# A block product scheme for one projection, weight sums on another engine, and an order between two engines' sums

## Chip, core and metric

The kernel runs on one core of a Trainium2 chip. The metric is device microseconds of one execution of the program. Three runs of the kernel before gave 254.39, 254.42 and 254.69 us, median 254.42.

## What is computed

```python
B, T, D, K, U = 2, 4000, 512, 5, 8
h = sum of K shifted einsums of x with w1;  h = gelu(h)[:, ::2, :]
f = sum of K shifted einsums of h with w2;  f = gelu(f)[:, ::2, :]
fe = jnp.einsum("btd,de->bte", f, w_f)
ge = jnp.einsum("bud,de->bue", g, w_g)
j = jnp.tanh(fe[:, :, None, :] + ge[:, None, :, :])
return jnp.einsum("btud,dv->btuv", j, w_o)
```

Two convolutions of five taps with stride 2 turn 4000 steps into 1000 per batch. The projected f (512 columns, "fe") is added to each of 8 projected rows of g, tanh is taken, and the product with w_o gives the output of 2 × 1000 × 8 × 512 values, the joint. Inputs and output are bf16.

## The kernel before

Channels lie on the 128 partitions in NK = 4 slices, time along the columns. Batch 0 is convolved first, then batch 1; the convolutions use sums of inputs and weights, so that fewer products are wanted, and each unit (one slice of 128 output channels of one stretch of time) runs through five steps s1 to s5 of one or two products. f of batch b is `fT[b]`, in three planes of NT3 = 334 columns (time modulo 3).

**The projection.** `fe(b, half, m)` takes 501 columns of f and one slice of 128 output channels: four matmuls into one PSUM bank, then one copy to `feT[b]` in float32, by VectorE (L810) for even m and by ScalarE (L480) for odd m. Batch 0 has eight such groups, which run one after another, with a tanh put behind each pair. `tanh` (ScalarE) reads all 1000 columns of one slice of `feT` and adds a column of `geT` as bias; it writes `jT` or, later, `jX`.

**The joint.** The output is made in 28 blocks of class `Seven` (four tiles of 128 rows each) and 13 single tiles of class `Plain`. `Seven` treats a block as a 2 × 2 product of halves and makes it from seven block products for eight: four sums of tanh blocks (`sums`, L980, tile `ss`), four sums of blocks of w_o (`wosums`, tile `tw`), seven products of four matmuls, three of whose accumulated states are kept in float32 (`sn`, L917 and L918) and added again on VectorE at the end (`og`, L475). The sums of w_o are made on GpSimd. Each sum in `sums` may go to VectorE or GpSimd, and evictions written with `evict(None, ...)` may go to ScalarE or VectorE.

**The order.** Instructions are noted as operations with reads, writes and a cost. `Plan.schedule` then lists them per engine: each engine takes an operation that is ready, TensorE and GpSimd the one noted first, VectorE and ScalarE the one with the earliest due time, and up to 150 changed due times are tried against the planner's own end. The order of the text is thus a priority, not an order of execution. `port` marks sums for which VectorE and GpSimd are taken to lock each other out: `lock` is the time at which the last one ends. Waits are put between engines as semaphores in `emit`, from the reads and writes, and from a list `after` of further operations.

**Pieces.** When the first projection is due, steps of batch 1's convolution are left: `conv` holds 26 of them (three of the unit at hand, fifteen of three more units, and the eight groups `fe(1, ...)`). `piece(n)` notes the next n. Before, one piece stands ahead of the first projection and three behind it; then the blocks of the joint take them by `fill`: two each in blocks 0 to 8, one each in 9 to 14, where there are any left.

**The start.** `turn` transposes a first part of x on TensorE; each call's two halves of the result are copied out to `eo`, the first by VectorE (L592), the second by ScalarE. `w1part` makes sums of the first convolution's weights on VectorE (`wu`, `ws`, `ssum`).

Of the kernel before, what the change touches and what calls it, by code (L numbers as in the profile page):

```python
# [10 lines left out]
FP16 = mybir.dt.float16  # L11
# [57 lines left out]
class Plan:  # L69
# [158 lines left out]
    def once(self, pred, succ, late, hold):  # L228


        ops, HOP, n = self.ops, self.HOP, len(self.ops)
        left = [len(p) for p in pred]
        ready = list(hold)
        free = {e: 0.0 for e in ("pe", "act", "dve", "pool", "sp")}
        cand = {e: [] for e in free}
        engines = [o.alt or (o.eng,) for o in ops]
        for i in range(n):
            if not left[i]:
                for e in engines[i]:
                    cand[e].append(i)  # L240
        order, where = {e: [] for e in free}, {}
        wire, lock, start, done = 0.0, 0.0, [0.0] * n, [0.0] * n
        for _ in range(n):
            best = None
            for e, c in cand.items():
                if c:
                    t = max(free[e], min(ready[i] for i in c))
                    if best is None or t < best[0]:
                        best = (t, e)
            t, e = best  # L250
            now = [i for i in cand[e] if ready[i] <= t + 0.02]
            i = min(now) if e in ("pe", "sp", "pool") else min(now, key=lambda i: (late[i], i))
            for f in engines[i]:
                cand[f].remove(i)
            order[e].append(i)
            o = ops[i]
            cost = o.cost
            if o.alt:
                where[i], cost = e, o.alt[e][1]
            start[i] = t  # L260
            free[e] = t + cost
            if o.port:
                if lock > t - 0.2 and e == "dve":
                    free[e] = max(t, lock) + cost + 0.2
                elif lock > t:
                    free[e] = lock + cost
                lock = free[e]
            done[i] = end = free[e]
            if o.dma:
                wire = max(wire, t + 1.8) + o.wire  # L270
                end = max(wire, t + 2.0) + o.slack
            for s in succ[i]:
                ready[s] = max(ready[s], end + HOP if pred[s][i] else free[e])
                left[s] -= 1
                if not left[s]:
                    for f in engines[s]:
                        cand[f].append(s)
        return max(free.values()), order, start, done, ready, where

    def emit(self, block, tail):  # L280
        nc, ops = self.nc, self.ops
        pred = self.edges()
        order = self.schedule(pred)
        pred = self.edges()
        pos = {i: p for e in order for p, i in enumerate(order[e])}
        deps = []
        for o in ops:
            need = {}
            for j, w in pred[o.idx].items():
                q = ops[j]  # L290
                if not w:
                    continue
                if q.dma:
                    need[("dma", j)] = j
                elif q.eng not in need or pos[need[q.eng]] < pos[j]:
                    need[q.eng] = j
            deps.append(need)
            for k, j in need.items():
                if not isinstance(k, tuple):
                    ops[j].signal = True  # L300
        cnt = {e: 0 for e in self.COMPUTE}
        sem = {e: nc.alloc_semaphore(f"s_{e}") for e in self.COMPUTE}
        for e in self.COMPUTE:
            for i in order[e]:
                if not ops[i].dma:
                    if ops[i].signal:
                        cnt[e] += 1
                    ops[i].count = cnt[e]

        def run(name, e):  # L310
            seen = {}

            def wait(s, v):
                if seen.get(id(s), 0) < v:
                    seen[id(s)] = v
                    e.wait_ge(s, v)

            for i in order[name]:
                o = ops[i]
                for k, j in sorted(deps[i].items(), key=lambda kj: -kj[1]):  # L320
                    if isinstance(k, tuple):
                        wait(ops[j].sem, ops[j].val)
                    else:
                        wait(sem[k], ops[j].count)
                ins = o.fn(e)
                if o.dma:
                    ins.then_inc(o.sem, 16)
                elif o.signal:
                    ins.then_inc(sem[name], 1)
            if name == "sp":  # L330
                for s, v in tail:
                    wait(s, v)

        @block.sync
        def _(e):
            run("sp", e)

        @block.gpsimd
        def _(e):
            run("pool", e)  # L340

        @block.tensor
        def _(e):
            run("pe", e)

        @block.scalar
        def _(e):
            run("act", e)

        @block.vector  # L350
        def _(e):
            run("dve", e)


def bass_standalone__seq2seq_rnn_t_joint__speech_kernel(
# [40 lines left out]
    with ExitStack() as es:  # L396
# [62 lines left out]
        assert ss[3].end <= xs[2].end and ss[7].end <= xs[1].end  # L459
        tw = at("tw", [4, 2, NT // 2], FP16, wg_sb.end - wg_sb.bytes)  # L460
        assert tw.end <= wg_sb.end
        ps = Psum(es.enter_context(nc.psum_tensor("acc", [P, 8 * NT], FP32)))
        block = es.enter_context(nc.Block(no_gpsimd_drain=True))
        pl = Plan(nc)
        sub, add = ALU.subtract, ALU.add

        def vec_cost(o, ins, fast=True):
            bf = fast and all(not v.psum and v.ap.dtype == BF16 for v in (o,) + tuple(ins))
            return o.ap.free_size() * (0.52e-3 if bf else 1.04e-3) + 0.065

        def memset(v):
# [2 lines left out]
        def tt(eng, o, a, b, op):  # L474
            pl.op(eng, lambda e: e.tensor_tensor(out=o.ap, in0=a.ap, in1=b.ap, op=op), (a, b), (o,),  # L475
                  0.02 + 2.14e-3 * o.ap.free_size() if eng == "pool" else vec_cost(o, (a, b)))
# [98 lines left out]
        def turn(rt, pp, cost):  # L575
            for h in range(2):
                bk = 4 * (rt ^ pp) + 2 * h + 1
                pv = View(psb[:, bk * 1024:bk * 1024 + 512].rearrange("p (r k c) -> p r k c", r=2, k=2), np.array([bk]), True)

                def fn(e, pv=pv, h=h):  # L580
                    for k in range(2):
                        for r in range(2):
                            ins = e.transpose(pv.ap[:, r, k, :], xr[rt].h[:, 2 * r + pp, 2 * h + k, :], ident.h[:, :])
                    return ins
                pl.op("pe", fn, (xr[rt][:], ident[:]), (pv,), cost)
                lo = 16 + 2 * P * rt
                o = eo[pp, 2 * h:2 * h + 2, lo:lo + 2 * P].map(lambda a: a.rearrange("p k (c r) -> p k c r", r=2))
                v = pv.map(lambda a: a.rearrange("p r k c -> p k c r"))
                if h:
                    act(o, v, ACT.Copy)  # L590
                else:
                    pl.op("dve", lambda e, o=o, v=v: e.tensor_copy(out=o.ap, in_=v.ap), (v,), (o,), vec_cost(o, (v,)))  # L592
# [208 lines left out]
        def fe(b, half, m):  # L801
# [7 lines left out]
            else:  # L809
                pl.op("dve", lambda e, o=o, v=v: e.tensor_copy(out=o.ap, in_=v.ap), (v,), (o,), vec_cost(o, (v,)))  # L810

        def slot(j):
            if j < XB:
                return jT, j % RING
            j = (j - XB) % (WIDE + RING)
            return (jX, j) if j < WIDE else (jT, j - WIDE)
# [23 lines left out]
                act(jcols(k, lo, n), feT[b][k, t:t + n], ACT.Tanh, bias=geT[k * BU + v:k * BU + v + 1])  # L840
                lo += n

        def wosums():
            h = NT // 2
            b11, b12, b21, b22 = (wo_sb[2 * k:2 * k + 2, c * h:(c + 1) * h] for k in range(2) for c in range(2))
            tt("pool", tw[0], b12, b11, sub)
            tt("pool", tw[1], b22, tw[0], sub)
            tt("pool", tw[2], b22, b12, sub)
            tt("pool", tw[3], b21, tw[1], sub)

        def tail_zero(b):
            v = hT[b][2:6, :, HOFF + NT3 - 1:HOFF + NT3]
# [9 lines left out]
        def steps(slot, i, lo, hi):  # L862
            when(slot, *[lambda w=w: trip[i].step(w) for w in STEPS[lo:hi]])
# [18 lines left out]
        when(17, load_late, lambda: tail_zero(1))  # L882
        steps(18, 5, 0, 4)
        steps(19, 5, 4, 13)
        when(20, ge)
        nu = 21
        for t in range(nu):
# [195 lines left out]
                    conv.pop(0)()  # L1083
                    far[0] = not conv

        wosums()
        first = [lambda h=h, m=m: fe(0, h, m) for m in range(NK) for h in range(2)]
        piece()
        for i, f in enumerate(first):
            f()  # L1090
            if i % 2:
                tanhs(0, 0, 1)
        piece(3)

        S1 = 15
        gaps = (1, 3, 5, 7)
# [78 lines left out]
```

## Time and profile before

| what | value |
|---|---|
| median of three runs | 254.42 us |
| profiled execution, its own time | 253.94 us |
| its span, first to last instruction | 252.2 us |
| granted TensorE clock | 1.00 |
| TensorE busy | 246.4 us |
| VectorE busy | 209.9 us |
| ScalarE busy | 210.0 us |
| GpSimd busy | 103.2 us |

PE is TensorE's matmuls, PEld its weight loads, DVE VectorE, ACT ScalarE, POOL GpSimd. Rows of a timeline give start, duration, engine, line, operation, out<-in, shapes and count; a bracket holds the idle time of the engine before it and what ended that. Since matmuls are pipelined, the spacing of their starts, not their duration, is what one of them takes of TensorE.

### The profile page before, as it was taken

The page shows a single profiled execution, that of the slowest core. Times are in us where ns is not written, and L with a number is a line of the kernel's source. Part 1 is how long each engine was busy: PE and PEld are TensorE (multiplying, and loading weights), DVE is VectorE, ACT ScalarE, POOL GpSimd, SP SyncE. Part 2 cuts the span into 40 slices and gives each one's busy share as a digit, 9 for nine tenths or more (in the row PEclk, how much of TensorE's full clock was granted, in tenths as well). Part 3 has the DMA queues.
Part 4 walks back from the last instruction along what each step waited for, and adds up shares of the span by engine and source line. Part 5 has one row for each costly group of instructions (what it writes and reads, how often), then busy time and mean ns, then how long its engine had stood idle before and what let it go on. Part 6 is the DMA issues. An engine that isn't in the chain of part 4 may idle for free.

```text
span 252.2 us, 5270 instructions
## 1 busy us (share of the span) xinstructions
PE 246.4 (98%) x1913; PEld 180.9 (72%) x1919; DVE 209.9 (83%) x342; ACT 210.0 (83%) x352; POOL 103.2 (41%) x107
## 2 busy tenths in 40 slices
PE   7999999999999999999999999999999999999994
PEld 3745977666666666667467878877778878787882
DVE  2699999956999998295546799799899999999783
ACT  4396998859869767884699999999999999998762
POOL 1000000000000000002418889698998999998500
PEclk9999999999999999999999999999999999999999
DMA  6999999989100043000002223332344446555646
GB/s 233 306 229 188 172 142 179 187 148 358 45 0 3 0 143 110 0 1 3 0 0 86 83 87 99 130 108 83 118 137 149 145 135 205 165 167 170 205 149 209
DMA packets 55159, 31.99 MB, mean 127 GB/s; under 512 B 32062, under 2 KB 54878, under 8 KB 55134
## 3 DMA queue, kind: packets, MB, share of 16 engines
q1 hardware_dynamic: 54846, 31.47, 47.6%
q8 instruction: 15, 0.25, 0.4%
q10 hardware_dynamic: 288, 0.20, 0.3%
q14 instruction: 10, 0.08, 0.1%
HBM read 7.86 MB, written 16.38 MB: 96 GB/s over the span
## 4 chain that ended last, share of the span: by engine, by line
PE 87%; DVE 5%; DMA 4%; ACT 1%; issue 1%; SPq 0%; DVEq 0%
PE acc L488 87%; DMA w_sb<-in_w_dram 4%; DVE wu L595 1%; DVE row L475 1%; DVE xa L475 1%; DVE ssum L475 1%; DVE w_t L475 1%; DVE og L475 1%; ACT row L480 0%; DVE w_x L475 0%; ACT w_x L480 0%; ACT sd L480 0%; ACT hT L480 0%; SPq L511 0%; ACT ost L480 0%
## 5 line engine op out<-in xcount | busy, mean ns | idle before, releaser
L475 DVE TENSOR_TENSOR og<-acc,sn 128x512 bf16<-128x512 f32 x84 | 55.6, 683 | 6.4 <-PE acc L488 4.4
L480 ACT ACTIVATE jT<-feT,geT 128x1000 bf16<-128x1000 f32 (+6 forms) x56 | 52.7, 1016 | 0.5 <-DVE feT L810 0.4
L488 PE MATMUL acc<-tw,ss 128*128 128x256 f16 x336 | 46.0, 273 | 0.0
L488 PE MATMUL acc<-row,w_sb 128*128 128x334 bf16 (+2 forms) x224 | 38.8, 296 | 0.0
L488 PEld LDWEIGHTS acc<-tw,ss 128*128 128x128 f16 x336 | 32.6, 98 | 7.8 <-ACT sn L917 0.4
L917 ACT ACTIVATE sn<-acc 128x512 f32<-128x512 f32 x54 | 34.8, 657 | 3.8 <-PE acc L488 3.5
L980 POOL TENSOR_TENSOR ss<-jT 128x512 f16<-128x512 bf16 x23 | 28.8, 1263 | 13.4 <-ACT jT L480 10.8
L488 PE MATMUL acc<-wo_sb,jT 128*128 128x256 bf16 (+1 forms) x187 | 31.5, 292 | 0.3
L488 PEld LDWEIGHTS acc<-row,w_sb 128*128 128x128 bf16 x224 | 21.0, 97 | 8.9 <-DVE acc L595 0.4
L480 ACT ACTIVATE jX<-feT,geT 128x1000 bf16<-128x1000 f32 (+4 forms) x28 | 26.2, 986 | 0.0
L472 POOL MEMSET hT<- 128x8 bf16 (+2 forms) x6 | 0.8, 148 | 61.6 <-ACT hT L480 44.1
L480 ACT ACTIVATE hT<-acc 128x334 bf16<-128x334 f32 (+3 forms) x36 | 15.5, 441 | 9.7 <-PE acc L488 9.7
L488 PEld LDWEIGHTS acc<-wo_sb,jT 128*128 128x128 bf16 x192 | 18.7, 98 | 6.2
L595 DVE SCALAR_TENSOR_TENSOR acc<-acc,sd 128x334 f32<-128x334 f32 (+2 forms) x24 | 11.6, 483 | 13.8 <-PE acc L488 13.7
L480 ACT ACTIVATE sd<-acc 128x334 f32<-128x334 f32 (+2 forms) x48 | 20.4, 433 | 3.2 <-PE acc L488 2.4
L918 DVE COPY sn<-acc 128x512 f32<-128x512 f32 x30 | 20.5, 685 | 2.4 <-PE acc L488 2.4
L475 DVE TENSOR_TENSOR row<-row 128x1336 bf16<-128x1336 bf16 (+2 forms) x24 | 19.0, 795 | 0.0
L980 POOL TENSOR_TENSOR ss<-jX 128x512 f16<-128x512 bf16 x15 | 17.4, 1171 | 1.2 <-ACT jX L480 0.6
L488 PE MATMUL acc<-hT,w_t 128*128 128x334 bf16 x96 | 17.6, 304 | 0.0
L488 PE MATMUL acc<-xp,w_t 128*128 128x334 bf16 (+1 forms) x96 | 17.4, 305 | 0.0
L488 PE MATMUL acc<-xp,w_x 128*128 128x334 bf16 (+1 forms) x96 | 16.9, 305 | 0.0
L488 PE MATMUL acc<-eo,w_sb 128*128 128x468 bf16 (+2 forms) x96 | 16.2, 328 | 0.6 <-ACT eo L480 0.6
(111 smaller groups left out, 511.2 us busy)
## 6 DMA issues: line engine op xcount, KB each, us to landing
out_dram<-og SPq DMA_DIRECT2D x98, 128.0 KB, 2.0
w_sb<-in_w_dram SPq DMA_DIRECT2D x10, 512.0 KB, 5.5
out_dram<-ost SPq DMA_DIRECT2D x10, 128.0 KB, 2.2
xr<-in_x_dram SPq DMA_DIRECT2D x2, 512.0 KB, 4.6
wf_sb<-in_w_f_dram SPq DMA_DIRECT2D x1, 512.0 KB, 3.6
wg_sb<-in_w_g_dram SPq DMA_DIRECT2D x1, 512.0 KB, 4.6
wo_sb<-in_w_o_dram SPq DMA_DIRECT2D x1, 512.0 KB, 5.7
xp<-in_x_dram SPq DMA_TRANSPOSE x18, 4.9
```

What stands on the lines that cost most here:

```text
L472: pl.op("pool", lambda e: e.memset(v.ap, 0.0), (), (v,))
L475: pl.op(eng, lambda e: e.tensor_tensor(out=o.ap, in0=a.ap, in1=b.ap, op=op), (a, b), (o,), 0.02 + 2.14e-3 * o.ap.free_size() if eng == "po ...
L480: pl.op("act", lambda e: e.activation(o.ap, i.ap, func, scale=scale, bias=0.0 if bias is None else bias.ap), rd, (o,), o.ap.free_size() * ...
L488: ins = e.matmul(o.ap, lhsT=l.ap, rhs=r.ap, start=start and n == 0, stop=stop and n == len(pairs) - 1, skip_group_check=not check)
L595: pl.op(eng, lambda e: e.scalar_tensor_tensor(out=o.ap, in0=a.ap, scalar=f, in1=b.ap, op0=ALU.mult, op1=add), (a, b), (o,), vec_cost(o, (a ...
L917: pl.flex({"act": (lambda e: e.activation(o.ap, v.ap, ACT.Copy), 0.05 + n * 0.833e-3), "dve": (lambda e: e.tensor_copy(out=o.ap, in_=v.ap) ...
L918: "dve": (lambda e: e.tensor_copy(out=o.ap, in_=v.ap), 0.065 + n * 1.04e-3)}, (v,), (o,))
L980: fn = lambda e, o=S[i], x=x, y=y, op=op: e.tensor_tensor(out=o.ap, in0=x.ap, in1=y.ap, op=op)
```

## The change

Batch 0's projection becomes two objects of class `FeSeven`, t = 0 and 1, each for two slices of the output (t and t + 2) and all 1002 columns in two overlapping halves of 504: seven products of two matmuls. It needs four sums of f (`fsums`, tile `sf`) and four of w_f (`wsums(twf, wf_sb)`), all on VectorE; three accumulated states per object are kept in float32 (`kf`) by `evict(None, ...)`, and three of four blocks are finished by an addition on VectorE. The sums of w_o move from GpSimd to VectorE by the same function. Nine pieces stand around the first projection: two ahead, three between the objects' products, four behind. In the planner, an engine's own sums no longer lock that engine, and sums of 16-bit floats cost VectorE less. Each port operation of GpSimd also waits for the latest port operation of VectorE that the plan starts up to 1.5 us before it. One of the copies to `eo` goes from VectorE to ScalarE.

```diff
-                if lock > t - 0.2 and e == "dve":
+                if owner != e and lock > t - 0.2 and e == "dve":
                     free[e] = max(t, lock) + cost + 0.2
-                elif lock > t:
+                elif owner != e and lock > t:
                     free[e] = lock + cost
-                lock = free[e]
+                lock, owner = free[e], e
...
+        near = None
+        for o in sorted((o for o in ops if o.port), key=lambda o: (self.start[o.idx], o.eng == "pool")):
+            if o.eng == "dve":
+                near = o.idx
+            elif near is not None and self.start[near] > self.start[o.idx] - 1.5:
+                o.after.append(near)
...
+        QH = NT3 // 2 + 1
+        twf = at("twf", [4, 2, NT // 2], FP16, wv[2].end - wv[2].bytes)
+        sf = at("sf", [4, 2, 3, QH], BF16, xt_off + 8192)
+        kf = [at(f"kf{i}", [3, QH], FP32, v.end - v.bytes) for i, v in enumerate(ssum + ws[:2])]
...
-            bf = fast and all(not v.psum and v.ap.dtype == BF16 for v in (o,) + tuple(ins))
+            bf = fast and all(not v.psum and v.ap.dtype in (BF16, FP16) for v in (o,) + tuple(ins))
...
-                if h:
+                if h or rt and pp:
                     act(o, v, ACT.Copy)
...
+        def fsums(b):
+            a = lambda r, k: fhalf(b, r, slice(2 * k, 2 * k + 2))
+            pl.port = True
+            tt("dve", sf[0], a(1, 0), a(1, 1), add)
+            tt("dve", sf[1], sf[0], a(0, 0), sub)
+            tt("dve", sf[2], a(0, 0), a(1, 0), sub)
+            tt("dve", sf[3], a(0, 1), sf[1], sub)
+            pl.port = False
...
+            def product(self, i, bk, start):
...
+                mm(ps.cols(bk * NT, 3 * QH), [(lhs(k), rhs(k)) for k in range(2)], start, True, False)
...
+            def p1(self):
+                self.A = take()
+                self.product(1, self.A, True)
+                self.s1 = self.keep(self.A)
...
+            def p6(self):
+                self.product(6, self.A, False)
+                self.u2 = self.keep(self.A)
+            def p7(self):
+                self.product(7, self.A, False)
+                self.out(1, 1, self.A, self.d5)
...
+            def p4(self):
+                self.product(4, self.A, False)
+                self.out(1, 0, self.A)
+                free.append(self.A)
...
-        def wosums():
+        def wsums(tw, w):
...
-            tt("pool", tw[0], b12, b11, sub)
...
+            tt("dve", tw[0], b12, b11, sub)
...
+        when(18, lambda: wsums(twf, wf_sb))
...
-        wosums()
-        first = [lambda h=h, m=m: fe(0, h, m) for m in range(NK) for h in range(2)]
-        piece()
-        for i, f in enumerate(first):
-            f()
-            if i % 2:
-                tanhs(0, 0, 1)
+        piece(2)
+        f0, f1 = FeSeven(0, 0), FeSeven(0, 1)
+        f0.p1()
+        f0.p2()
+        fsums(0)
+        wsums(tw, wo_sb)
+        f1.p1()
+        f0.p5()
+        f1.p2()
+        f0.p6()
+        f1.p5()
+        f0.p7()
+        f0.p3()
+        f0.p4()
+        tanhs(0, 0, 1)
         piece(3)
+        f1.p6()
+        f1.p7()
+        f1.p3()
+        f1.p4()
+        tanhs(0, 0, 3)
+        piece(4)
```

More of the change, by code (lines that the diff above doesn't have):

```diff
@@ L241, in once @@
         order, where = {e: [] for e in free}, {}
-        wire, lock, start, done = 0.0, 0.0, [0.0] * n, [0.0] * n
+        wire, lock, owner, start, done = 0.0, 0.0, None, [0.0] * n, [0.0] * n
         for _ in range(n):
@@ L461, in bass_standalone__seq2seq_rnn_t_joint__speech_kernel @@
         assert tw.end <= wg_sb.end
+        QH = NT3 // 2 + 1
+        twf = at("twf", [4, 2, NT // 2], FP16, wv[2].end - wv[2].bytes)
+        sf = at("sf", [4, 2, 3, QH], BF16, xt_off + 8192)
+        kf = [at(f"kf{i}", [3, QH], FP32, v.end - v.bytes) for i, v in enumerate(ssum + ws[:2])]
+        assert twf.end <= wv[3].end and sf.end <= xt[0].end and 3 * QH <= NT
         ps = Psum(es.enter_context(nc.psum_tensor("acc", [P, 8 * NT], FP32)))
@@ L810, in fe, with fhalf @@
                 pl.op("dve", lambda e, o=o, v=v: e.tensor_copy(out=o.ap, in_=v.ap), (v,), (o,), vec_cost(o, (v,)))
+        def fhalf(b, r, k):
+            q0 = r * (NT3 - QH)
+            return fT[b][k, :, q0:q0 + QH]
+        def fsums(b):
[6 more added lines that the diff above has]
+            pl.port = False
@@ new lines, in bass_standalone__seq2seq_rnn_t_joint__speech_kernel, with __init__, keep, out @@
+        class FeSeven:
+            def __init__(self, b, t):
+                self.b, self.t = b, t
+            def product(self, i, bk, start):
+                h, lo = NT // 2, self.t * P
+                rhs = {1: lambda k: fhalf(self.b, 0, k), 2: lambda k: fhalf(self.b, 0, 2 + k),
+                       4: lambda k: fhalf(self.b, 1, 2 + k)}.get(i)
+                if rhs is None:
+                    si = {5: 0, 6: 1, 7: 2, 3: 3}[i]
+                    rhs = lambda k: sf[si, k]
+                lhs = {1: lambda k: wf_sb[k, lo:lo + P], 2: lambda k: wf_sb[2 + k, lo:lo + P],
+                       3: lambda k: wf_sb[2 + k, h + lo:h + lo + P]}.get(i)
+                if lhs is None:
+                    ti = {5: 0, 6: 1, 7: 2, 4: 3}[i]
+                    lhs = lambda k: twf[ti, k, lo:lo + P]
+                mm(ps.cols(bk * NT, 3 * QH), [(lhs(k), rhs(k)) for k in range(2)], start, True, False)
+            kept = 0
+            def keep(self, bk):
+                v = kf[FeSeven.kept % len(kf)]
+                FeSeven.kept += 1
+                evict(None, v[:].map(lambda a: a.rearrange("p r q -> p (r q)")), ps.cols(bk * NT, 3 * QH))
+                return v
+            def out(self, r, c, bk, v=None):
+                q = NT3 // 2
+                cut = lambda a: a[:, :, r:r + q].rearrange("p r q -> p q r")
+                p = ps.cols(bk * NT, 3 * QH).map(lambda a: cut(a.rearrange("p (r q) -> p r q", r=3)))
+                o = feT[self.b][2 * c + self.t, 3 * r * q:3 * (r + 1) * q].map(lambda a: a.rearrange("p (q r) -> p q r", r=3))
+                if v is None:
+                    evict(None, o, p)
+                else:
+                    tt("dve", o, p, v[:].map(cut), add)
+            def p1(self):
+                self.A = take()
+                self.product(1, self.A, True)
+                self.s1 = self.keep(self.A)
+            def p2(self):
+                bk = take()
+                self.product(2, bk, True)
+                self.out(0, 0, bk, self.s1)
+                free.append(bk)
+            def p5(self):
+                self.D = take()
+                self.product(5, self.D, True)
+                self.d5 = self.keep(self.D)
+            def p6(self):
[4 more added lines that the diff above has]
+                self.out(1, 1, self.A, self.d5)
+            def p3(self):
+                self.product(3, self.D, False)
+                self.out(0, 1, self.D, self.u2)
+                free.append(self.D)
+            def p4(self):
+                self.product(4, self.A, False)
+                self.out(1, 0, self.A)
+                free.append(self.A)
@@ L841, in tanh @@
                 lo += n
-        def wosums():
+        def wsums(tw, w):
             h = NT // 2
-            b11, b12, b21, b22 = (wo_sb[2 * k:2 * k + 2, c * h:(c + 1) * h] for k in range(2) for c in range(2))
-            tt("pool", tw[0], b12, b11, sub)
-            tt("pool", tw[1], b22, tw[0], sub)
-            tt("pool", tw[2], b22, b12, sub)
-            tt("pool", tw[3], b21, tw[1], sub)
+            b11, b12, b21, b22 = (w[2 * k:2 * k + 2, c * h:(c + 1) * h] for k in range(2) for c in range(2))
+            pl.port = True
+            tt("dve", tw[0], b12, b11, sub)
+            tt("dve", tw[1], b22, tw[0], sub)
+            tt("dve", tw[2], b22, b12, sub)
+            tt("dve", tw[3], b21, tw[1], sub)
+            pl.port = False
         def tail_zero(b):
```

## The prediction

> **What bounds the kernel now.** I read the page's busy times first, then TensorE's waits, then busy time by stretch, and last the timeline around the projection, at the start, and at the sums.
>
> ```profile
> PE 246.4 (98%) x1913; PEld 180.9 (72%) x1919; DVE 209.9 (83%) x342; ACT 210.0 (83%) x352; POOL 103.2 (41%) x107
> PEclk9999999999999999999999999999999999999999
> PE acc L488 <- DVE zero L495: 1.2, 1, 1.2
> PE acc L488 <- ACT eo L480: 0.6, 2, 0.4
> PE acc L488 <- ACT sd L480: 0.3, 1, 0.3
> ```
>
> TensorE is busy for 246.4 of 252.2 us at full clock, and only 2.1 us of its waiting has a name, all before 28 us. By stretch (duration, then busy time and count of PE, PEld, DVE, ACT, POOL, then clock, DMA share, GB/s):
>
> ```profile
> 117.00:120.50 3.50, 3.50 (x39) 2.50 (x38) 0.01 (x1) 1.25 (x4) 2.19 (x2) 1.00 0.00 0
> 120.50:130.00 9.50, 9.50 (x53) 4.94 (x51) 4.08 (x7) 7.87 (x12) 2.35 (x3) 1.00 0.00 0
> 130.00:140.00 10.00, 9.95 (x78) 7.45 (x77) 7.64 (x14) 10.00 (x17) 7.80 (x7) 1.00 0.16 54
> 140.00:160.00 20.00, 20.00 (x168) 15.90 (x166) 18.13 (x28) 19.64 (x35) 17.82 (x16) 1.00 0.29 93
> 160.00:180.00 20.00, 20.00 (x160) 15.30 (x158) 17.64 (x29) 20.00 (x33) 16.74 (x15) 1.00 0.37 119
> 180.00:200.00 20.00, 20.00 (x172) 16.42 (x170) 19.21 (x32) 20.00 (x32) 18.59 (x17) 1.00 0.39 125
> 200.00:220.00 20.00, 19.84 (x163) 16.04 (x165) 18.74 (x31) 20.00 (x34) 19.94 (x18) 1.00 0.53 172
> 220.00:240.00 20.00, 19.95 (x172) 16.67 (x171) 17.91 (x29) 16.98 (x28) 15.35 (x14) 1.00 0.55 179
> ```
>
> From 117 to 240 us TensorE idles for 0.26 us (0.05, 0.16 and 0.05). So every matmul less is worth its own spacing, and there is nothing else to win there. But ScalarE is full from 130 to 220 us (0.36 us idle of 90), VectorE idles 8.6 us there, and GpSimd is full from 200 to 220. All four engines run abreast: TensorE has the end, with a small margin to the others. Work added to ScalarE and VectorE must therefore go where they have room, which is 117 to 130 us: VectorE idles 3.49 + 5.42 = 8.9 us there and ScalarE 2.25 + 1.63 = 3.9.
>
> **The projection.** These are its rows, with what stands before and behind it (start, duration):
>
> ```profile
> 119.41 0.45 ACT L480 ACTIVATE fT<-acc 128x334 bf16<-128x334 f32 x1 [0.93 <-PE acc L488]
> 120.35 6.99 PE L488 MATMUL acc<-fT,wf_sb 128*128 128x501 bf16 x32
> 121.52 1.42 DVE L810 COPY feT<-acc 128x501 f32<-128x501 f32 x2
> 122.97 1.13 ACT L480 ACTIVATE jT<-feT,geT 128x1000 bf16<-128x1000 f32 x1 [0.39 <-DVE feT L810]
> 127.17 0.73 PE L488 MATMUL acc<-row,w_sb 128*128 128x334 bf16 x4
> 127.74 0.73 PE L488 MATMUL acc<-hT,w_sb 128*128 128x334 bf16 x4
> 130.01 0.38 PE L488 MATMUL acc<-wo_sb,jT 128*128 128x256 bf16 x2
> ```
>
> The 32 matmuls begin at 120.35 and the next work at 127.17: 6.82 us, 213 ns each. The change has 2 × 7 × 2 = 28, of 504 columns: 213 × 504 / 501 = 214.4 ns, together 6.00 us. That is 0.82 us less on the path that sets the end. The Trainium skill, TensorE: Matmul & The Clock Gate, Back-to-back issue gap, gives a sustained spacing of about 131 ns for 512 columns; four fewer would then bring an estimated 0.52 us. The 213 ns here disagree, and I keep 0.82.
>
> **What VectorE and ScalarE get.** Costs come from these groups (last but one: busy us, mean ns):
>
> ```profile
> L475 DVE TENSOR_TENSOR og<-acc,sn 128x512 bf16<-128x512 f32 x84 | 55.6, 683 | 6.4 <-PE acc L488 4.4 <-ACT sn L917 1.7
> L480 ACT ACTIVATE jT<-feT,geT 128x1000 bf16<-128x1000 f32 x32 | 36.3, 1191 | 0.4 <-DVE feT L810 0.4
> L917 ACT ACTIVATE sn<-acc 128x512 f32<-128x512 f32 x54 | 34.8, 657 | 3.8 <-PE acc L488 3.5 <-DVE og L475 0.3
> L475 DVE TENSOR_TENSOR row<-row 128x1336 bf16<-128x1336 bf16 x16 | 13.5, 850 | 0.0
> L475 DVE TENSOR_TENSOR w_t<-w_sb 128x512 bf16<-128x512 bf16 x12 | 5.0, 419 | 0.0
> ```
>
> Each row block reads PSUM seven times, 14 in all against 8: six more VectorE additions of 504 columns at 683 × 504 / 512 = 672 ns, 4.0 us; the other eight cost what the eight copies cost. The four sums of f have 1008 elements; between 419 ns (512) and 850 ns (1336) that is 0.68 us each, 2.7 us. The eight sums of w_f and w_o are 512 long: 8 × 0.42 = 3.4 us. Together 10.1 us, in 12.8 us of room. The sums of w_o leave GpSimd:
>
> ```profile
> 118.31 2.27 POOL L475 TENSOR_TENSOR tw<-wo_sb 128x512 f16<-128x512 bf16 x2 [17.37 <-PE acc L488]
> 120.54 2.39 POOL L475 TENSOR_TENSOR tw<-wo_sb,tw 128x512 f16<-128x512 bf16 x2
> ```
>
> That was idle time of GpSimd: its 2.35 us between 120.5 and 130 are these sums and nothing else, so nothing is won. They cannot start before the g projection has let go of the buffer, which is when GpSimd began, 118.3; VectorE idles from 117 to 120.5, so they and those of w_f fit there. Cost: nothing; without that cover they would stand 3.4 us ahead of the sums of f.
>
> The sums of f wait for the last block of f, out at 119.41 + 0.45 = 119.86 (their buffer lies on planes that the convolution's last products read, which are done by then), and end near 119.9 + 2.7 = 122.6. TensorE arrives at the first of them (product 5) later than now by one more convolution piece: two groups of four, 0.57 us apart as 127.17 and 127.74 show, 1.13 us. So it starts the projection at 121.5, and product 5 after three products of 0.43, at 122.8. The first sum is ready at 120.6. No stall.
>
> **The joint's start.** Nine convolution pieces stand in and around the projection for four. The five more are four pieces of two groups and one of one, 4 × 1.13 + 0.57 = 5.1 us that TensorE does earlier. Now the first full tanh runs at 122.97, because copies of blocks come out one after another. In the new order a block is complete only after product 4, behind the chain product 6, eviction, product 7, addition, product 4, eviction: 3 × (0.43 + 0.17 to the result + 0.67 + 0.1) = 4.1 us from 123.6, so 127.7 us. It begins 4.7 us later, while the first joint product moves from 130.01 by 5.1 − 0.8 to 134.3. The lead shrinks only by about 0.4 us, plus what pieces and evictions take from ScalarE between; I take one tanh of 1.1 us. The second row block starts three pieces (2.8 us) behind the first, is complete near 132.4, and two tanhs are wanted from it: 134.7 against 134.3. TensorE takes the lowest ready number, so other pieces can fill this. Bounds: 0 to 1.1 us; I take 0.3, as the 0.26 us idle of now is the nearest row.
>
> **The start of the kernel.** One copy of turned x goes from VectorE to ScalarE.
>
> ```profile
> 14.00:28.00 14.00, 13.57 (x101) 8.50 (x100) 14.00 (x30) 11.67 (x25) 0.35 (x3) 1.00 0.99 201
> 8.07 1.29 DVE L592 COPY eo<-acc 128x512 bf16<-128x512 bf16 x2 [1.93 <-PE acc L583]
> 10.70 0.69 DVE L595 SCALAR_TENSOR_TENSOR wu<-w_sb,wu 128x512 f32<-128x512 bf16 x1
> 11.43 0.63 ACT L480 ACTIVATE w_x<-wu 128x512 bf16<-128x512 f32 x1 [2.06 <-DVE wu L595]
> 24.95 0.27 PEld L488 LDWEIGHTS acc<-row,w_x 128*128 128x128 bf16 x4 [0.36 <-ACT sd L480]
> 27.24 0.27 PEld L488 LDWEIGHTS acc<-row,w_t 128*128 128x128 bf16 x4 [0.50 <-ACT sd L480]
> ```
>
> VectorE gets half of 1.29, 0.65 us, back; ScalarE has 2.06 us idle before 11.43. From 14 to 28 us VectorE has no pause at all (14.00 of 14), and TensorE, idle for 0.43 us of it, waits at 24.95 and 27.24 for sums that ScalarE copies from that work. Bounds 0 and 0.6 us (VectorE moves by 0.65 at most); I take 0.3, between the two, and no loss, because ScalarE idles where the copy goes.
>
> **GpSimd behind VectorE.** All joint sums by engine, and three meetings:
>
> ```profile
> 126.00:240.00 114.00, 21.31 (x30) 96.24 (x82) 1.00 0.39 126
> 134.51 0.43 DVE L980 TENSOR_TENSOR ss<-jT 128x512 f16<-128x512 bf16 x1 [0.57 <-ACT jT L480]
> 134.55 1.39 POOL L980 TENSOR_TENSOR ss<-jT 128x512 f16<-128x512 bf16 x1 [0.89 <-ACT jT L480]
> 152.17 1.16 POOL L980 TENSOR_TENSOR ss<-ss,jT 128x512 f16<-128x512 f16 x1
> 152.21 1.40 DVE L980 TENSOR_TENSOR ss<-jT,ss 128x512 f16<-128x512 bf16 x1
> ```
>
> The 30 sums on VectorE took 21.31 us; at the 0.43 of the undisturbed one they would take 12.9, so 8.4 us are waiting. At 152.17 GpSimd was 40 ns ahead and VectorE's sum took 1.40, 0.97 too long. The new wait turns such a meeting round: VectorE regains up to 0.97, GpSimd and the sums queued behind it (and the products 5, 6, 7 and 3 that read them) come about 0.5 later. Where VectorE is first anyway, as at 134.51, GpSimd was already held (1.39 for 1.16), and the semaphore's way is added, 0 to 0.2 us. The Trainium skill, SBUF — State Buffer, SBUF: two separate sides, says that the one that starts first keeps the shared ports for its whole instruction; by that rule the wait can pay only in such races, not in every meeting, and both pairs agree with it. On the path I put this at zero: bounds −0.5 (VectorE's regained time removes the small gaps) and +0.5 (GpSimd has 0.06 us spare from 200 to 220).
>
> **Sum.** 253.94 − 0.82 − 0.30 + 0.30 = 253.1 us for the profiled execution. It lies 0.48 us under the median of 254.42, so the median becomes 253.6, 0.32% less. The measurement tells about 0.2%, 0.5 us.
>
> **Rivals.** *The joint runs short of cover (slower).* The pieces done early are missing later: 26 pieces less nine last to block 8 of the joint, where now the blocks 9 to 12 still have one each, a projection of the second batch. Two groups of the joint's products give the spacing:
>
> ```profile
> 136.63 1.04 PE L488 MATMUL acc<-tw,ss 128*128 128x256 f16 x8
> 137.50 0.60 PE L488 MATMUL acc<-wo_sb,jT 128*128 128x256 bf16 x4
> ```
>
> Eight matmuls take 137.50 − 136.63 = 0.87 us, 0.109 each. A block of seven products without a piece is 28 × 0.109 = 3.05 us of TensorE. ScalarE and VectorE need seven evictions at 0.67, four tanhs of 512 columns at 1.13 / 1000 and 30 / 28 sums at 0.71: 4.7 + 2.3 + 0.8 = 7.8, or 3.9 each. A projection piece has TensorE for 4 × 0.213 = 0.85 and them for 0.33 each, so it covers 0.52. Four make 2.1 us; with the lead that is 1.1 short, 3.2. Full price: 253.6 − 0.3 + 3.2 = 256.5. For it: ScalarE's 20.00 of 20. Against: VectorE's 8.6 us idle in 130 to 220, the 8.4 us it loses in meetings, and ScalarE's 3.0 us idle after 220. It decides from 1.1 us on (then nothing is won), and counts as slower from 1.6 us, half its price.
>
> *The hand-over eats it (no change).* The second row block's tanhs come late by the upper bound of 1.1 us and no other piece is ready: 253.6 − 0.3 + 1.1 = 254.4. Against: five more pieces can be pulled forward.
>
> *More is won.* The start gives 0.6, the hand-over costs nothing, VectorE's regained time gives 0.5: 254.42 − 0.82 − 0.6 − 0.5 = 252.5. For it: 8.4 us of waiting in sums. Against: the wait only turns races.
>
> **Chances.** Forecast 0.47 (its own range 253.1 to 253.9), more won 0.10, hand-over 0.13, short of cover 0.30: its price must be paid by more than half, and VectorE's idle time of the same size stands against that. Faster by over 0.2% 0.57, within 0.13, slower 0.30. The range leaves out the lowest of more won and the top of the cover rival, about 0.15 together: 252.6 to 256.3.
>
> **What would show it.** Right: 28 matmuls of 504 columns near 6.0 us in sum; the first product with w_o near 134; TensorE still idle below 0.6 us from 117 us to 240; the starts' waits at 25 and 27 us smaller; no joint sum on VectorE above 1.3 us that began within 0.1 us of GpSimd's. Wrong: TensorE's idle time in 180 to 240 us above 1 us, released by ScalarE's jT or sums on GpSimd (cover); a gap of about 1 us just before the first product with w_o (hand-over); VectorE's sums of w_f behind 122 us.

## The result: 1.0 us less

The changed kernel takes 253.39 us (median of six runs, 253.09 to 253.62) against 254.40 for the kernel before beside it: ratio 0.996, 95% interval 0.9947 to 0.9972. That is 0.2 us under the forecast of 253.6. Run again later it gave 253.30, ratio 0.9959 (0.9945 to 0.9974).

The profiled execution took 253.50 us, its span 251.7. The busy times and TensorE's waits after:

```profile
PE 246.3 (98%) x1909; PEld 180.3 (72%) x1915; DVE 211.8 (84%) x354; ACT 211.7 (84%) x356; POOL 97.5 (39%) x105
PE acc L499 <- DVE zero L506: 1.2, 1, 1.2
PE acc L594 <- DMA xr<-in_x_dram: 0.3, 1, 0.3
PE acc L499 <- ACT eo L491: 0.2, 1, 0.2
PE acc L499 <- ACT sd L491: 0.2, 1, 0.2
```

VectorE and ScalarE together are busy 3.6 us more, although 10.1 us were added; 3.8 us of the difference are in VectorE's sums of the joint (17.54 us for 21.31, row below), the rest was not traced. By stretch (columns as before):

```profile
14.00:28.00 14.00, 13.84 (x103) 8.56 (x101) 14.00 (x30) 11.84 (x25) 0.36 (x3) 1.00 0.94 196
117.00:120.50 3.50, 3.50 (x40) 2.52 (x38) 2.73 (x7) 1.60 (x5) 0.00 (x0) 1.00 0.00 0
120.50:130.00 9.50, 9.50 (x56) 4.96 (x55) 8.39 (x15) 6.50 (x12) 0.00 (x0) 1.00 0.00 0
130.00:140.00 10.00, 9.95 (x70) 6.64 (x70) 6.50 (x12) 10.00 (x16) 4.91 (x5) 1.00 0.09 28
200.00:220.00 20.00, 19.84 (x162) 15.85 (x164) 15.72 (x28) 20.00 (x36) 17.68 (x16) 1.00 0.56 181
220.00:240.00 20.00, 19.89 (x170) 16.49 (x170) 17.31 (x29) 18.56 (x31) 15.91 (x15) 1.00 0.50 163
```

VectorE's gap from 117 to 130 us is filled (11.12 of 13 us busy for 4.09), and TensorE idles as little as before: 0.32 us from 117 to 240, for 0.26. Most of that is not idle time in either kernel: the pages count 1909 matmuls for 1915 weight loads here and 1913 for 1919 before, so six matmuls lack a record; a second trace of the changed kernel (`after_again`) has 1915 of both, and TensorE idles 0.05 us there in these stretches. Three fixed points place the gain: the second transposes, the g projection and the last full group of matmuls. First the kernel before, then the changed one, with the rows around its projection and its first full tanh:

```profile
7.65 1.05 PE L583 MATMUL acc<-ident,xr 128*128 128x128 bf16 x16
117.68 0.55 PE L488 MATMUL acc<-gT,wg_sb 128*128 128x16 bf16 x16
247.53 1.46 PE L488 MATMUL acc<-wo_sb,jT 128*128 128x512 bf16 x8
```

```profile
8.10 1.05 PE L594 MATMUL acc<-ident,xr 128*128 128x128 bf16 x16 [0.28 <-DMA xr<-in_x_dram]
118.03 0.55 PE L499 MATMUL acc<-gT,wg_sb 128*128 128x16 bf16 x16
120.70 1.01 PE L499 MATMUL acc<-fT,wf_sb 128*128 128x504 bf16 x4
121.55 0.73 PE L499 MATMUL acc<-row,w_sb 128*128 128x334 bf16 x4
126.82 2.15 ACT L491 ACTIVATE jT<-feT,geT 128x1000 bf16<-128x1000 f32 x2 [0.28 <-DVE feT L486]
133.77 0.81 PE L499 MATMUL acc<-wo_sb,jT 128*128 128x512 bf16 x3
247.20 1.46 PE L499 MATMUL acc<-wo_sb,jT 128*128 128x512 bf16 x8
```

In this execution TensorE waited for x to land and began these transposes 0.45 us later. From the transposes to the g projection it took 109.93 us for 110.03; from there to the last group 129.17 for 129.85, which is 0.68 us less; and from the last group to the end of the span 4.50 for 4.67. With the late start that makes the 0.5 us between the two spans. Four matmuls of 504 columns take 0.85 us from start to start of what follows (120.70 to 121.55), 0.2125 each; 28 make 5.95 for 6.82, so 0.87 us was saved, and 0.19 of it was given back between the g projection and the last group. The order differs from the text: the second of the two pieces noted ahead ran behind the first four matmuls of the projection.

### The profile page after: what moved, and what is told of

The parts are those of the page before. It is cut to its first block, busy times and chain, and to the rows that moved or that the text cites. A ratio compares the mean times of both kernels' runs of the same rounds, so it can differ in the third digit from the quotient of the medians.

```text
span 251.7 us, 5281 instructions
## 1 busy us (share of the span) xinstructions
PE 246.3 (98%) x1909; PEld 180.3 (72%) x1915; DVE 211.8 (84%) x354; ACT 211.7 (84%) x356; POOL 97.5 (39%) x105
## 4 chain that ended last, share of the span: by engine, by line
PE 73%; ACT 16%; issue 4%; DMA 4%; SPq 1%; DVE 1%; POOL 0%; ACTq 0%; DVEq 0%
PE acc L499 73%; ACT sn L1016 4%; DMA xr<-in_x_dram 3%; ACT jX L491 2%; ACT jT L491 2%; ACT row L491 2%; ACT sd L491 1%; ACT og L1016 1%; DMA xe<-in_x_dram 1%; SPq L529 1%; ACT ost L1016 1%; ACT hT L491 1%; DVE og L486 1%; ACT xp L491 0%; PE acc L594 0%
## 5 line engine op out<-in xcount | busy, mean ns | idle before, releaser
L486 DVE TENSOR_TENSOR og<-acc,sn 128x512 bf16<-128x512 f32 x84 | 55.0, 684 | 10.6 <-PE acc L499 8.9
L1016 ACT ACTIVATE sn<-acc 128x512 f32<-128x512 f32 x51 | 33.1, 655 | 2.6 <-PE acc L499 1.7
L491 ACT ACTIVATE jX<-feT,geT 128x1000 bf16<-128x1000 f32 (+4 forms) x28 | 25.2, 970 | 0.0
L1017 DVE COPY sn<-acc 128x512 f32<-128x512 f32 x33 | 22.2, 684 | 2.7 <-PE acc L499 2.4
L491 ACT ACTIVATE sd<-acc 128x334 f32<-128x334 f32 (+2 forms) x48 | 19.7, 431 | 3.5 <-PE acc L499 2.8
L606 DVE SCALAR_TENSOR_TENSOR acc<-acc,sd 128x334 f32<-128x334 f32 (+2 forms) x24 | 11.6, 483 | 10.1 <-PE acc L499 10.0
L1079 POOL TENSOR_TENSOR ss<-jX 128x512 f16<-128x512 bf16 x16 | 18.5, 1159 | 3.5 <-DVE ss L1079 3.5
L499 PE MATMUL acc<-wo_sb,ss 128*128 128x256 bf16 x112 | 17.0, 273 | 0.0
```

The source lines that it names most:

```text
L491: pl.op("act", lambda e: e.activation(o.ap, i.ap, func, scale=scale, bias=0.0 if bias is None else bias.ap), rd, (o,), o.ap.free_size() * ...
L499: ins = e.matmul(o.ap, lhsT=l.ap, rhs=r.ap, start=start and n == 0, stop=stop and n == len(pairs) - 1, skip_group_check=not check)
L606: pl.op(eng, lambda e: e.scalar_tensor_tensor(out=o.ap, in0=a.ap, scalar=f, in1=b.ap, op0=ALU.mult, op1=add), (a, b), (o,), vec_cost(o, (a ...
L1016: pl.flex({"act": (lambda e: e.activation(o.ap, v.ap, ACT.Copy), 0.05 + n * 0.833e-3), "dve": (lambda e: e.tensor_copy(out=o.ap, in_=v.ap) ...
L1017: "dve": (lambda e: e.tensor_copy(out=o.ap, in_=v.ap), 0.065 + n * 1.04e-3)}, (v,), (o,))
L1079: fn = lambda e, o=S[i], x=x, y=y, op=op: e.tensor_tensor(out=o.ap, in0=x.ap, in1=y.ap, op=op)
```

## Experiments

All times below are medians, with the kernel before on the same chip at 254.29 to 254.33. `no_order` and `one_wait` keep the plan of the changed kernel, `order_only` that of the kernel before. The other kernels are planned anew (`seven_alone` and `seven_order` alike), so their difference to the changed kernel holds what another plan brings; `own_lock` (below) gives one size of that for the same work, 0.45 us.

**One part undone each.** `eight_back` puts the first projection back, with its four pieces, and without the sums of f and w_f:

```diff
-        when(18, lambda: wsums(twf, wf_sb))
-        piece(2)
-        f0, f1 = FeSeven(0, 0), FeSeven(0, 1)
...
+        wsums(tw, wo_sb)
+        first = [lambda h=h, m=m: fe(0, h, m) for m in range(NK) for h in range(2)]
+        piece()
...
```

`no_order` removes the loop over port operations in `emit`; `no_turn` has `if h:` in `turn` again.

> The changed kernel once more, beside the three kernels with one part undone. Ratio to the kernel before near 0.996 (1.0 us less).

> The changed kernel with only the first projection back to eight groups (32 matmuls of 501 columns, four pieces in front, no sums of f and w_f); the ordering of the sums, the sums of w_o on VectorE, the planner and the copy at the start stay changed. If the four matmuls saved are the gain: 0.8 to 0.9 us slower than the changed kernel, so about 254.2, within 0.2 us of the kernel before. Rival, that the gain comes from the ordering and the plan: it stays within 0.3 us of the changed kernel.

> The changed kernel without the waits of GpSimd's sums on VectorE's; the plan is the same. Prediction's value: the waits are worth nothing on the path, so within 0.3 us of the changed kernel. VectorE's sums begun just behind one of GpSimd's come back at about 1.4 us, GpSimd's own idle time in front of sums falls. Rival, that the turned races carry the gain: 0.5 to 1 us slower, with TensorE idle more between 140 and 240 us.

> The changed kernel with the one copy of turned x back on VectorE. By the prediction 0.3 us slower (TensorE's waits at 25 and 27 us come back); by the trace after, in which the way from the second transposes to the g projection is only 0.1 us shorter than before, 0.1 us or nothing.

Measured: 253.30 (after_again), 253.71 (eight_back, ratio 0.998, 0.9968 to 0.9992), 254.56 (no_order, 1.001, 1.0001 to 1.002) and 253.44 (no_turn, 0.9968, 0.9958 to 0.9977). So neither view was right alone. The projection with its pieces is worth 0.4 us in this company, half of what its matmuls save; its interval and that of `after_again` just overlap, and the two traces differ the same way, by 0.51 us from the g projection to the last group (129.68 for 129.17). The waits are worth 1.26 us, although they remove no work; the copy at the start 0.14, which the intervals do not tell from nothing. The trace of `no_order` has one place that explains the waits. These are VectorE, GpSimd and TensorE there:

```profile
205.36 3.56 DVE L1073 TENSOR_TENSOR ss<-jT,ss 128x512 f16<-128x512 bf16 x1
208.84 1.87 DVE L480 TENSOR_TENSOR og<-acc,sn 128x512 bf16<-128x512 f32 x3
204.13 2.29 POOL L1073 TENSOR_TENSOR ss<-jT 128x512 f16<-128x512 bf16 x2
206.36 1.17 POOL L1073 TENSOR_TENSOR ss<-ss,jT 128x512 f16<-128x512 f16 x1
207.47 1.17 POOL L1073 TENSOR_TENSOR ss<-jT 128x512 f16<-128x512 bf16 x1
209.58 0.61 PE L493 MATMUL acc<-tw,jT 128*128 128x256 f16 x4 [1.19 <-DVE og L480]
```

A sum of VectorE began at 205.36, about 0.1 us behind the second of GpSimd's two, and ended at 208.92, behind that one and GpSimd's next two: 3.56 us for 0.42. Three additions (`og`) queue behind it; they let go of PSUM banks, and TensorE waited 1.19 us. That one wait is about the size of the whole loss of 1.26.

**Is it that one meeting?** `one_wait` is `no_order` with a single wait, for the operation of GpSimd behind VectorE's 28th marked sum:

```diff
+        near, seen = None, 0
+        for o in sorted((o for o in ops if o.port), key=lambda o: (self.start[o.idx], o.eng == "pool")):
+            if o.eng == "dve":
+                near, seen = o.idx, seen + 1
+            elif seen == 28 and self.start[near] > self.start[o.idx] - 1.5:
+                o.after.append(near)
```

`order_only` is the kernel before with the full ordering and nothing else.

> The kernel without the ordering, plus one single wait of the 28: the sum on GpSimd that ran just ahead of VectorE's sum at 205.4 us (which then took 3.56 us there) waits for it. If that one meeting carries what the ordering is worth: within 0.3 us of the changed kernel (253.3), and TensorE's wait of 1.2 us at 209 us is gone. If the worth is spread over many meetings: it stays at 254.2 or above.

> The kernel before with the ordering of GpSimd's sums alone, same plan. It has no sum on VectorE above 1.4 us and no wait of TensorE behind one, so if the ordering only guards against such a meeting: within 0.3 us of the kernel before. If VectorE's waiting in sums costs the kernel time as such: 0.5 us faster or more.

Measured: 253.35 (ratio 0.9964, 0.9949 to 0.9978) and 254.32 (0.9999, 0.999 to 1.0008). One wait brings back all of it, and in the kernel before, which has no such meeting, the ordering is worth nothing. In `one_wait` VectorE goes first at that place:

```profile
204.85 0.41 DVE L1079 TENSOR_TENSOR ss<-jT,ss 128x512 f16<-128x512 bf16 x1
207.57 1.43 DVE L1079 TENSOR_TENSOR ss<-jT 128x512 f16<-128x512 bf16 x1
205.34 1.15 POOL L1079 TENSOR_TENSOR ss<-jT 128x512 f16<-128x512 bf16 x1 [0.54 <-DVE ss L1079]
```

The next sum, at 207.57, still loses 1.0 us to GpSimd, and costs the kernel nothing. All joint sums by engine (VectorE, then GpSimd) point the same way. First the changed kernel, then `no_order`, then `one_wait`:

```profile
126.00:240.00 114.00, 17.54 (x27) 92.53 (x82) 1.00 0.38 123
```

```profile
126.00:240.00 114.00, 23.22 (x27) 94.20 (x82) 1.00 0.38 123
```

```profile
126.00:240.00 114.00, 21.08 (x27) 95.87 (x84) 1.00 0.38 124
```

Between the first two lie 5.7 us of VectorE's time. `one_wait` returns only 2.1 of it and is as fast, so the other meetings cost the kernel nothing that these runs can tell.

**The projection alone, and what it meets.** `seven_alone` is the kernel before with `FeSeven`, its sums and pieces; `seven_order` adds the ordering; `wo_on_gpsimd` is the changed kernel with

```diff
-        wsums(tw, wo_sb)
+        wsums(tw, wo_sb, 'pool')
```

> The kernel before with the seven-product projection alone (with its sums of f and w_f on VectorE and nine pieces around it); the sums of w_o on GpSimd, no ordering, the planner's old lock, the copy on VectorE. If the projection is the gain: 0.7 to 0.9 us faster than the kernel before. If it needs VectorE's time that the ordering gives back: under 0.4 us faster.

> The kernel before with the seven-product projection and the ordering, but the sums of w_o on GpSimd, the old lock and the copy on VectorE. If the projection alone lost 1.3 us at the one meeting near 206 us and about 1 us beside the sums of w_o: the first comes back, 254.2 to 254.5, still no faster than the kernel before.

> The changed kernel with the four sums of w_o back on GpSimd. By the prediction (GpSimd was idle there, nothing won): within 0.2 us of the changed kernel. By the trace of the projection alone, in which two sums of f took 1.22 us beside them for 0.68 and TensorE waited near 121.6 and 127.4: 0.5 to 1 us slower, with those waits.

Measured: 255.62 (ratio 1.0053, 1.0039 to 1.0067), 254.39 (1.0005, 0.9995 to 1.0014) and 254.33 (0.9998, 0.9989 to 1.0007). Alone, the scheme with four matmuls fewer is 1.3 us slower; the ordering returns 1.2; and the sums of w_o off GpSimd are worth 1.0 us in the changed kernel. The trace of `wo_on_gpsimd` (VectorE, GpSimd, TensorE) shows how:

```profile
117.73 0.55 PE L499 MATMUL acc<-gT,wg_sb 128*128 128x16 bf16 x16
119.95 1.23 DVE L486 TENSOR_TENSOR sf<-fT 128x1008 bf16<-128x1008 bf16 x1 [2.29 <-ACT fT L491]
123.11 1.22 DVE L486 TENSOR_TENSOR sf<-fT,sf 128x1008 bf16<-128x1008 bf16 x1
120.59 3.19 POOL L486 TENSOR_TENSOR tw<-wo_sb,tw 128x512 f16<-128x512 bf16 x2
121.65 0.74 PE L499 MATMUL acc<-row,w_sb 128*128 128x334 bf16 x4 [0.24 <-DVE acc L606]
127.51 0.60 PE L499 MATMUL acc<-fT,twf 128*128 128x504 bf16 x2 [0.43 <-DVE feT L486]
134.44 0.81 PE L499 MATMUL acc<-wo_sb,jT 128*128 128x512 bf16 x3
```

Two sums of f take 1.22 us beside GpSimd's sums of w_o, and VectorE is late for a convolution step and for an addition of the projection. From the g projection to the first product with w_o this kernel takes 16.71 us, the changed one 15.74 (118.03 to 133.77), and 0.67 of the 0.97 us between them is idle time at these two places. From there to the last group both take 113.4 us, so the whole loss lies here. GpSimd's sums of w_o are not marked as port operations in this kernel and stand outside the ordering; whether ordering them would have done as well as moving them was not tested. In the changed kernel both sets are on VectorE, in its idle time, and the same sum is short:

```profile
118.61 0.76 DVE L486 TENSOR_TENSOR tw<-wo_sb 128x512 f16<-128x512 bf16 x2 [0.66 <-PE acc L499]
119.29 0.88 DVE L486 TENSOR_TENSOR tw<-wo_sb,tw 128x512 f16<-128x512 bf16 x2
120.24 0.68 DVE L486 TENSOR_TENSOR sf<-fT 128x1008 bf16<-128x1008 bf16 x1
```

**Cover.** `pieces4` has `piece(1)`, `piece(1)`, `piece(2)` for 2, 3, 4. `seven_both` replaces the second batch's eight groups by two more `FeSeven` objects, with buffers of their own:

```diff
-        conv += [lambda h=h, m=m: fe(1, h, m) for m in range(NK) for h in range(2)]
+        g0, g1 = FeSeven(1, 0), FeSeven(1, 1)
+        def second():
+            fsums(1)
+            g1.p1()
+        conv += [g0.p1, g0.p2, second, g0.p5, g1.p2, g0.p6, g1.p5, g0.p7, g0.p3, g0.p4, g1.p6, g1.p7, g1.p3, g1.p4]
```

`own_lock` takes `owner != e` out of the planner's two conditions.

> The changed kernel with four pieces around the projection as before (one, one, two) for nine. The five pieces are then noted behind, in the joint. If pieces are pulled forward by readiness anyway: within 0.3 us of the changed kernel. If their place is what hides the chain of product, eviction, product, addition: TensorE waits up to 2 us between 122 and 136 us, and it is 0.5 to 2 us slower.

> The changed kernel with the second batch's projection in seven products too (buffers in the planes of h that are free by then). TensorE does another four matmuls less, 0.87 us. ScalarE and VectorE get six additions and four sums more, 4.0 + 2.7 us, at a place where ScalarE is full and VectorE idles 0.15 to 1.6 of 20 us. If TensorE alone sets the end: 0.8 us faster than the changed kernel. If the room of the two others decides, as the prediction has it: they lack up to 3.3 us each less what idle time is near, TensorE idles 1 to 3 us between 160 and 240, and it is 0 to 2.5 us slower than the changed kernel.

> The changed kernel with the planner's old rule, by which an engine's own last sum also makes its next one longer. Another plan of the same work: if the plan's prices of sums matter little, within 0.3 us of the changed kernel; if the new prices move sums to where they belong, 0.5 us slower or more.

Measured: 255.00 (ratio 1.0029, 1.0018 to 1.004), 255.83 (1.006, 1.0046 to 1.0073) and 253.75 (0.9977, 0.9966 to 0.9987). With four pieces TensorE waits at the hand-over for the tanhs of the second row block; the row is TensorE's in `pieces4`:

```profile
132.87 2.11 PE L499 MATMUL acc<-wo_sb,jT 128*128 128x512 bf16 x11 [1.45 <-ACT jT L491]
```

With the scheme in both batches, four more matmuls are saved and the kernel is 2.5 us slower than the changed one. Its busy times by stretch:

```profile
200.00:220.00 20.00, 19.34 (x157) 15.30 (x159) 16.82 (x27) 20.00 (x35) 16.16 (x15) 1.00 0.48 156
220.00:240.00 20.00, 19.75 (x161) 14.68 (x160) 18.36 (x28) 20.00 (x32) 16.23 (x15) 1.00 0.49 159
```

ScalarE is now full up to 240 us (18.56 of 20 in the changed kernel, 16.98 before), and TensorE idles 0.66 and 0.25 us in the two stretches, where the changed kernel's rows have 0.16 and 0.11. But most of what the span grew by stands behind TensorE's last matmul. These are `seven_both`'s rows (SPq is SyncE's queue, which sends out the results), and then the last one of the changed kernel:

```profile
117.67 0.55 PE L499 MATMUL acc<-gT,wg_sb 128*128 128x16 bf16 x16
243.99 4.44 DVE L486 TENSOR_TENSOR og<-acc,sn 128x512 bf16<-128x512 f32 x7
248.86 0.60 PE L499 MATMUL acc<-wo_sb,jT 128*128 128x256 bf16 x4
245.72 4.65 SPq L1037 DMA_DIRECT2D out_dram<-og  x10
251.99 0.45 SPq L1037 DMA_DIRECT2D out_dram<-ost  x1
```

```profile
249.09 0.44 SPq L1031 DMA_DIRECT2D out_dram<-ost  x1
```

Counted from the g projection, TensorE's last matmul ends 1.2 us later than in the changed kernel (117.67 to 249.46, for 118.03 to 248.66). The span, 254.5 us here and 251.7 there, then lasts another 5.0 us for 3.0. VectorE makes seven additions in a row up to 248.43, and the queue sends without a pause from 245.72 to 252.44; in the changed kernel it ends at 249.53. That the late additions hold up the results is argued from these rows, not tested. The planner's old rule, another plan of the same work, costs 0.45 us against 253.30; the two intervals just overlap.

## Why the prediction came out right

**The matmuls.** 0.82 us stood in the sum; 0.87 was saved at their place. One took 0.2125 us, where 0.2144 was worked out.

**VectorE's and ScalarE's work.** Most of it fitted into 117 to 130 us as forecast, with sums of f at 0.68 us; the sums of w_f ran well ahead, from 98.5 to 101.4 us, and one sum of f at 116.50. But the step "so nothing is won" for the sums of w_o was wrong: moving them is worth 1.0 us. I asked whether GpSimd had idle time there, and not which of VectorE's new instructions would run beside it. Left on GpSimd, they meet the sums of f, as `wo_on_gpsimd` shows.

**The hand-over.** The first full tanh came at 126.8 us (127.7 forecast), the first product with w_o at 133.77 (134.3), with no wait before it beyond 0.05 us of idle time in 130 to 140. The way behind the projection gave back 0.19 us for the 0.30 taken. The 0.30 leaned on 0.26 us of idle time that are mostly missing records, so that the two are close is luck. That pieces can be pulled forward does not replace their place: with four of them the hand-over rival comes true, at 1.45 us.

**The start.** 0.30 was taken. TensorE did idle less from 14 to 28 us (0.16 us for 0.43), but the way from the transposes to the g projection became only 0.10 shorter, and in the traces of `no_turn` and `order_only`, which have the copy on VectorE, it takes 109.78 and 109.79 us, less than the 109.93 here. Undoing the copy costs 0.14, within the noise. So no run shows a gain of the copy, and this term was too large by 0.2 to 0.3 us.

**The ordering.** Zero was taken, between −0.5 and +0.5; its worth is 1.26 us, outside the bounds. The nearest rows (1.40 us for 0.43) were the worst meetings of the plan of before. The new plan has one of 3.56 us, at a place where three additions and TensorE wait behind it. The Trainium skill, SBUF — State Buffer, SBUF: two separate sides, on which the step leaned, says that the loser is held for the winner's whole instruction; in `no_order` it was held for three. The other part of the step holds: turning the rest of the meetings wins nothing. The zero was also right for the kernel before, which has no such meeting (`order_only`); the step left out that the projection brings one.

**Short of cover.** The rival of 0.30 did not come true in the changed kernel: ScalarE used 1.6 us of its idle time after 220 us, and VectorE's sums became 3.8 us shorter in all (27 of them 17.54, where 30 took 21.31). It is what happens in `seven_both`.

So the number was met and the account was not: I gave the whole gain to the matmuls and the start. The runs show a scheme that alone costs 1.3 us, and two protections, the ordering (1.2) and the sums of w_o on VectorE (1.0), without which it is no gain. I foresaw neither of the two losses, and the parts that prevent them stood in my sum at nothing. That the sum still came within 0.2 us is in large part luck. What stays open is why the change without the projection (`eight_back`) is already 0.6 us faster than the kernel before: the ordering alone is worth nothing there, and the other parts were not run one by one without the projection. Its trace shows 0.17 us of it between the g projection and the last group (129.68 for 129.85).

## What to carry to other kernels

Where two engines share something, check new work not only for idle time on its engine, but for what the other engine does in the same microseconds. One wait that decides a race can be worth more than matmuls saved, but only where a queue stands behind the loser: find that place in the trace before ordering everything. Count what a cheaper product scheme adds to the engines that read its results: the same scheme won 0.4 us where they had room, and a second one, where ScalarE was full, lost 2.5.

## What was not expected of the hardware

A sum of VectorE (0.42 us when undisturbed) that began 0.1 us behind one of GpSimd's waited out three of them in a row, 3.56 us, in `no_order`, and 3.54 us at the same place of the joint in `seven_alone`, which has no ordering either:

```profile
206.08 3.54 DVE L1073 TENSOR_TENSOR ss<-jT,ss 128x512 f16<-128x512 bf16 x1
```

At 152.21 us in the kernel before and at 211.49 in `one_wait` (1.40 and 1.37 us), GpSimd's next sum followed at once as well, and VectorE came in after the first one, so being passed over is not the rule:

```profile
211.49 1.37 DVE L1079 TENSOR_TENSOR ss<-jT,ss 128x512 f16<-128x512 bf16 x1
```

VectorE began 0.04 and 0.06 us behind GpSimd in these two, 0.11 in the two long ones; what decides it was not tested.
